# Operands of seven weight blocks made on GpSimd during attention, and the last rows' operands on GpSimd alone

## The chip, the cores and the metric

The kernel runs on one core of a Trainium2 chip. Times are device microseconds of a whole execution, "us" throughout. Engines are named as the profile names them: PE (TensorE matmul; PEld its weight loads), DVE (VectorE), ACT (ScalarE), POOL (GpSimd) and SP (SyncE, which here only issues transfers). "L970" is line 970 of the kernel before.

## The reference

One block of a transformer with 2048 rows of 576, modulated by a condition vector:

```python
mod = (silu(c) @ w_mod).reshape(1, 6, 1, -1)
sa, ca, ga, sb, cb, gb = (mod[:, 0], ..., mod[:, 5])
h = layernorm(x) * (1 + ca) + sa
x = x + ga * attention(h, wqkv, wo)      # 32 heads of 18, full softmax over 2048 keys
h = layernorm(x) * (1 + cb) + sb
g, u = h @ w_gate, h @ w_up              # 576 x 4608 each
return x + gb * ((sigmoid(g) * u) @ w_down)
```

Everything is float32.

## The kernel before, in words

**Precision by splitting.** Matrix products run on operands in the float32r type. An operand is split into a high part (a copy, rounded to float32r) and a low part (the operand less its high part), and a product is the sum of high x high, high x low and low x high. Much of ACT's, DVE's and POOL's work is such splitting.

**Stages.** First come layer norm and the projections to q, k and v. Then attention: 32 units, each a pair of heads for one half of the query rows (16 units a half), and 16 steps to a unit, so 512 steps. A step has matmuls for the row maxima of units to come, reduced on DVE (`maxima`, L415); score matmuls, whose exponentials ACT takes (L881); and value matmuls (`values`, L501). At a unit's end ACT copies the accumulated output to a buffer `oT` (`taken`, L515), PE transposes it, and POOL scales it into the row tile (`outputs`, L544).

The order in which a step's work is issued is written out by hand (`STEPS`), and during attention PE follows the program's order exactly (`manual_schedule`, L841). Other work is spread over the steps by generators, each advanced by one piece with `next`:

- `down_parts` (L775), steps 64 to 240: POOL multiplies each block of `w_down` by the gate vector, splits it and stores it in DRAM (`wds`).
- `first_rows`, steps 240 to 437: the output projection of the first 1024 rows, their second layer norm, and their operands for the gated unit, on POOL (`operand_parts`).
- `last_rows_project`, from step 437: most of the output projection of the last 1024 rows.

A load issued in these generators is tied with `paced` to the exponential of the step in which it stands, so that it doesn't start earlier.

**The gated unit.** Gate and up weights are taken in 18 blocks of 256 columns. A block's four quarters (A11, A12, A21, A22: two halves of the inner dimension by two halves of the columns) enter seven products instead of eight, in the order `ORDER = (1, 6, 2, 7, 5, 4, 3)`; products 5, 6, 7 and 3 need sums and differences of quarters. Each product is 14 matmuls of 512 columns (`product`, L979), seven for gate and seven for up. The loop runs twice over the 18 blocks: first for the first 1024 rows, then for the last 1024. At the first two products of a block the block before is multiplied with its down weights (`down`, L1015, 48 matmuls each), and DVE adds the results into the row tile (L1019), which frees PE's accumulator.

In the first half of the rows every block's operands are made as it goes (`weights_operand`, three products ahead, `LOOK = 3`): SP loads the raw weights (`load_block`), POOL makes the sums (L959), ACT copies the high part (L970), DVE subtracts the low part (L971, and L972 for the 64 partitions of the last, narrow slice of the inner dimension), and SP stores the finished operand in DRAM (`ws`, L973). In the second half the operands are only loaded from `ws` (L949).

While the first half runs, `last_rows` (L1059) brings the last 1024 rows up to the same point, one piece at every second product: the rest of the output projection (`od` loaded, transposed, L1098 on PE, `x1d` stored), the second layer norm (rows loaded into `z`, transposed by L663, spilled to `hs`), and the operands of the seven products (`operand_parts`: four blocks `B` loaded from `hs`; POOL subtracts, L690; ACT copies the high part, L679; DVE subtracts the low part, L681 and L686; SP stores to `xs`). At the first half's last block these operands replace the first half's in SBUF.

Up to product 56 (`ORDERED`) of the gated unit the framework's scheduler chooses PE's order, and after it the program's order holds. Each engine works through its queue in order, and so does each queue that issues transfers.

Of the kernel before, what the change touches and what calls it, by code (L numbers as in the profile page):

```python
# [23 lines left out]
P = 128  # L24
# [19 lines left out]
NB = F // 256  # L44
LAG = 2
# [6 lines left out]
def tile_block(ctx, tc, x_in, wqkv, wo, w_gate, w_up, w_down, c_in, w_mod, out):  # L52
# [33 lines left out]
    def load_mod(a, b, i):  # L86

        cols = slice(2 * D * i, 2 * D * (i + 1))
        for t in range(0, 4, 2):
            rows = slice(t * P, (t + 2) * P)  # L90
            nc.sync.dma_start(a[:, t : t + 2, :], w_mod[rows, cols].rearrange("(t p) c -> p t c", p=P))
        nc.sync.dma_start(b[0:64, :], w_mod[DM:D, cols])
        return [a[:, t, :] for t in range(4)] + [b]
# [218 lines left out]
    with tc.tile_pool(name="ln", bufs=2) as ln:  # L312
# [23 lines left out]
        with tc.tile_pool(name="wmp", bufs=1) as wmp:  # L336
            zs = normalized(0)
            wm = wmp.tile([P, 5, 2 * D], F32, name="wm")
            wm = load_mod(wm[:, 0:4, :], wm[:, 4, :], 0)
# [147 lines left out]
    bgp = bgs.enter_context(tc.tile_pool(name="bgp", bufs=1))  # L487
# [320 lines left out]
    def load_block(pool, b, k, tied=None):  # L808
# [4 lines left out]
        raw = pool.tile([P, 2, 3, 256], F32, name=f"raw{k}", bufs=1 + k)  # L813
        queue = nc.gpsimd if tied else nc.sync
# [10 lines left out]
        return raw  # L825
# [18 lines left out]
    downs = down_parts()  # L844
    for u in range(UNITS):
# [6 lines left out]
        for kt in range(NT):  # L852
# [31 lines left out]
            if u in (1, 3):  # L884
                if kt == 2:
                    a = big.tile([P, 8, 640], F32, name="big")
                    a = a.rearrange("p a b -> p (a b)")[:, 0 : 8 * D].rearrange("p (t c) -> p t c", t=4)
                    b = slots.tile([P, 2560], F32, name="w0")[:, 0 : 2 * D]
                    mods = load_mod(a, b, 1 + u // 2)
                    row = slots.tile([P, 2560], F32, name="w1")[:, 0:384]  # L890
# [4 lines left out]
            if 4 * NT <= step < FROM0 and step % 2 == 0:  # L895
                next(downs, None)
            if step == FROM0:
                for _ in downs:
                    pass
# [5 lines left out]
            if u == 30 and kt == 7:  # L905
                first = [load_block(raws, 0, k, paced) for k in range(2)]
# [4 lines left out]
            if u == UNITS - 1 and kt == 9:  # L911
# [5 lines left out]
                for i in range(2):  # L917
                    X[5 + i] = both[:, i]
                    load_x(5 + i)
    while pending:  # L920
        values()
# [20 lines left out]
    def weights_operand(st, k):  # L942
# [3 lines left out]
        kept = ws[st["b"], ORDER.index(k)]  # L946
        flat = w.rearrange("p v a c -> p (v a c)").bitcast(F32)
        if st["half"] == 1:
            nc.sync.dma_start(flat, kept.bitcast(F32))  # L949
            return  # L950
# [10 lines left out]
        if k == 6:  # L961
            put("S1", A21, A22, ALU.add)
            put("S2", st["S1"], A11, ALU.subtract)
# [267 lines left out]
```

## Time and profile before

| | us |
|---|---|
| median of three runs | 2938.05 |
| lowest, highest | 2929.16, 2941.33 |
| the profiled execution | 2936.12 |
| its span, first to last instruction | 2934.3 |
| PE busy | 2867.2 |
| DVE busy | 2305.1 |
| ACT busy | 1497.6 |
| POOL busy | 614.7 |

The profile is of one execution. Its page gives busy time by engine, the span in 40 slices, the queues of the transfers, the chain of work that ended last, and the costliest groups of instructions. The trace behind it answers for any stretch, line or tile. Busy time of PE is modelled, since matmuls overlap; a group's mean is the mean duration of one instruction, which may overlap the next one's, so that count by mean is more than the busy time. In a chain of waits each row is a start, a length and what the time went to.

### The profile page before, as it was taken

The numbers are of one execution on the slowest core, as the hardware profiler recorded it, in microseconds if no ns is written. First come the engines' busy times: TensorE is split into PE (matmuls) and PEld (weight loads), VectorE is DVE, ScalarE is ACT, GpSimd is POOL, SyncE is SP. The second block draws the span as 40 slices with busy tenths as digits, with TensorE's granted clock in tenths as the row PEclk, the third lists the DMA queues.
The fourth block names the chain that finished last, engine by engine and source line by source line (L and its number), as shares of the span: only waits on it lengthen the run. The fifth ranks groups of instructions, "written<-read, shape, count | busy, mean of one in ns | idle before, by whom it ended". The sixth has DMA issues, their size and how long they took to land.

```text
span 2934.3 us, 46129 instructions
## 1 busy us (share of the span) xinstructions
PE 2867.2 (98%) x17141; PEld 1884.6 (64%) x17141; DVE 2305.1 (79%) x4021; ACT 1497.6 (51%) x2779; POOL 614.7 (21%) x793
## 2 busy tenths in 40 slices
PE   7999999999999999999999999998999999999999
PEld 6974333333334443443443788887888888888888
DVE  7278999999999999999992778888777555555555
ACT  3217778888887678878778333333332111111111
POOL 2001024444213110661102222233221100000000
PEclk9999999999999999999999999999999999999999
DMA  5333113333212110221125866686556854444443
GB/s 170 119 138 115 63 58 134 126 116 112 83 50 70 31 50 19 95 92 60 48 78 185 280 217 231 232 278 242 204 201 225 303 177 168 166 168 169 158 158 137
DMA packets 136089, 420.25 MB, mean 143 GB/s; under 512 B 18805, under 2 KB 56441, under 8 KB 123577
## 3 DMA queue, kind: packets, MB, share of 16 engines
q1 hardware_dynamic: 120472, 338.35, 33.7%
q0 software_dynamic: 15392, 78.95, 7.6%
q8 instruction: 135, 2.21, 0.3%
q14 instruction: 90, 0.73, 0.1%
HBM read 261.13 MB, written 155.59 MB: 142 GB/s over the span
## 4 chain that ended last, share of the span: by engine, by line
PE 85%; DVE 5%; ACT 4%; issue 3%; DMA 2%; SPq 1%; POOL 0%; ACTq 0%; DVEq 0%; POOLq 0%
PE o L501 17%; PE d L1015 14%; PE s L877 13%; PE x L979 13%; PE s L411 9%; PE bg L979 4%; PE bu L979 4%; PE s L267 4%; ACT p L881 3%; PE s L301 2%; PE s L638 2%; DVE w L971 1%; PE s L525 1%; DMA B<-hs 1%; DVE u L1163 0%
## 5 line engine op out<-in xcount | busy, mean ns | idle before, releaser
L415 DVE TENSOR_REDUCE mx<-s 128x1 f32<-128x512 f32 x2048 | 1266.9, 681 | 43.9 <-PE s L411 35.3
L881 ACT ACTIVATE p<-s 128x512 f32<-128x512 f32 x2048 | 1066.9, 607 | 268.7 <-PE s L411 145.4
L411 PE MATMUL s<-k,q 54*128 54x512 f32 x1920 | 658.0, 441 | 2.6 <-ACT p L881 1.0
L877 PE MATMUL s<-q,k 56*128 56x512 f32 x1920 | 581.5, 433 | 6.3 <-ACT p L881 0.4
L877 PEld LDWEIGHTS s<-q,k 56*128 56x128 f32 x1920 | 277.6, 185 | 469.5 <-DVE mx L415 292.6
L501 PE MATMUL o<-p,vaug 128*32 128x512 f32 x4096 | 554.4, 606 | 0.0
L1015 PE MATMUL d<-wd,hh 128*128 128x288 f32 x2304 | 470.9, 298 | 20.9 <-DVE Oa L1019 20.3
L1015 PEld LDWEIGHTS d<-wd,hh 128*128 128x128 f32 x2304 | 375.7, 189 | 35.8 <-DVE Oa L1019 27.2
L411 PEld LDWEIGHTS s<-k,q 54*128 54x128 f32 x1920 | 312.1, 185 | 80.5 <-ACT p L881 37.4
L1019 DVE TENSOR_TENSOR Oa<-Oa,d 128x288 f32<-128x288 f32 x576 | 255.9, 452 | 128.2 <-PE d L1015 123.1
L1015 PE MATMUL d<-wd,hl 128*128 128x288 f32 x1152 | 342.0, 297 | 0.0
L979 PE MATMUL x<-k,w 128*128 128x512 f32 x1008 | 245.5, 394 | 4.7 <-ACT w L970 2.4
L1015 PEld LDWEIGHTS d<-wd,hl 128*128 128x128 f32 x1152 | 218.1, 189 | 0.0
L979 PEld LDWEIGHTS x<-k,w 128*128 128x128 f32 x1008 | 188.8, 190 | 43.2 <-DVE u L1190 3.5
L991 ACT ACTIVATE u<-u 128x512 f32<-128x512 f32 x72 | 45.5, 631 | 318.7 <-DVE u L1179 312.7
L501 PEld LDWEIGHTS o<-p,vaug 128*32 128x32 f32 x4096 | 83.6, 108 | 163.7 <-issue 147.7
L988 ACT ACTIVATE sg<-x 128x512 f32<-128x512 f32 x36 | 21.5, 598 | 309.4 <-PE x L979 309.4
L1021 POOL DMA_DIRECT2D out_dram<-Oa x16 | 8.7, 542 | 606.5 <-DVE Oa L1019 606.5
L979 PE MATMUL x<-big,w 128*128 128x512 f32 x504 | 120.6, 390 | 1.0 <-issue 1.0
L979 PE MATMUL x<-w,w 128*128 128x512 f32 x504 | 121.0, 390 | 0.0
L267 PE MATMUL s<-hT,wq_h 128*128 128x512 f32 x324 | 106.1, 399 | 1.9 <-DVE hT L204 1.2
L979 PEld LDWEIGHTS x<-big,w 128*128 128x128 f32 x504 | 94.3, 188 | 21.0 <-issue 1.4
(221 smaller groups left out, 3345.2 us busy)
## 6 DMA issues: line engine op xcount, KB each, us to landing
ws<-w SPq DMA_DIRECT2D x126, 640.0 KB
w<-ws SPq DMA_DIRECT2D x126, 640.0 KB
wd<-wds SPq DMA_DIRECT2D x36, 1152.0 KB
wds<-w POOLq DMA_DIRECT2D x18, 1152.0 KB, 4.5
k<-qk SPq DMA_DIRECT2D x60, 288.0 KB
qk<-pl SPq DMA_DIRECT2D x32, 512.0 KB
w<-in_B_w_down_dram POOLq DMA_DIRECT2D x18, 576.0 KB, 4.9
q<-qk SPq DMA_DIRECT2D x64, 144.0 KB
```

The source lines that it names most:

```text
L267: nc.tensor.matmul(acc, w, hT[:, t, cols], start=n == 0, stop=n == len(ts_) - 1)
L301: nc.tensor.matmul(acc[:, 0:HALF], hT[:, k, rows], w, start=n == 0, stop=n == len(ts_) - 1,)
L411: nc.tensor.matmul(sp, qs[rows, qt * P : (qt + 1) * P], ks[rows, kc * 512 : (kc + 1) * 512], start=True, stop=True,)
L415: nc.vector.tensor_reduce(mx[:, h * n + qt, kc : kc + 1], sp, axis=AX.X, op=ALU.max)
L501: nc.tensor.matmul(acc[32 * j : 32 * j + 32, :], vaug[:, kt, (2 * p + h) * VW : (2 * p + h) * VW + 32], probs[2 * c + h], start=kt == 0, s ...
L638: nc.tensor.matmul(acc[:, :HALF], a, w, start=i == 0, stop=i == len(ts_) - 1)
L877: nc.tensor.matmul(sT, ks[rows, kcols], qs[rows, c * 512 : (c + 1) * 512], start=True, stop=True)
L881: state["exp"] = nc.scalar.activation(pr, sT, AF.Exp, scale=SCALE)
L979: nc.tensor.matmul(acc[v], w[:, v, a, :], X[s][:, b, :], start=first and n == 0, stop=n == 6, skip_group_check=not first,)
L991: nc.scalar.activation(t[:, 0:512], t[:, 0:512], AF.Sigmoid)
L1015: nc.tensor.matmul(acc[:, :HALF], a[:, f, rows], w[:, f, cols], start=n == 0, stop=n == 5)
L1019: nc.vector.tensor_add(Oa[:, t, cols], Oa[:, t, cols], acc[:, :HALF])
```

## The change

1. **Seven blocks' operands during attention** (`AHEAD = 7`). A new generator `operands()` runs on POOL, one operand at a piece: at every third step up to step 64, then at every sixth step up to 240. It loads a block's two raw tiles through POOL's queue into the room that `big` has before the second half's outputs need it, makes the sums, the high copy and both low subtractions on POOL, in a tile `w` of which there are two in turn, and stores to `ws`. In the gated unit the blocks 0 to 6 then load their operands in the first half of the rows too; the first three are loaded at the end of attention, into the raw tiles' room.
2. **Room for it.** The modulation weights (`load_mod`), which used `big`, go to `w0`, `w1` and a temporary. The pool `bgp` is opened at step 240 only; before that its place holds `opp`, with the operand tiles and a second `oT` for every other unit of the first half up to unit 12.
3. **Blocks 7 to 17.** The sum for product 7 is made at product 7 and no longer at product 6; the 64-partition subtraction moves from DVE to POOL.
4. **Last rows.** `operand_parts` runs on POOL alone, and its loads and stores are on POOL's queue; the loads are issued two turns before their use. The rows `xt` are loaded one ahead, and the loads of `z` a turn before the statistics. The pieces come at every product from 5 to 32 and then at two of three, where they came at every second.

The core of the diff:

```diff
+AHEAD = 7
...
-        oT = epool.tile([P, 512], F32, name="oT")
+        pool = opp if half == 0 and p % 2 and p < FROM0 // NT - 2 else epool
+        oT = pool.tile([P, 512], F32, name="oT")
...
+    def operands():
+        room = big.tile([P, 8, 640], F32, name="big").rearrange("p a b -> p (a b)")
...
+        def load(b, k):
+            if b < AHEAD:
+                fill_block(raw[k], b, k, nc.gpsimd, paced)
+        load(0, 0)
+        load(0, 1)
+        yield
+        for b in range(AHEAD):
+            for k, src, op, a, c in (
+                (7, S3, ALU.subtract, A11, A21), (1, A11, None, None, None),
+                (5, S2, ALU.add, A21, A22), (6, S2, ALU.subtract, S2, A11),
+                (3, S2, ALU.subtract, A12, S2), (2, A12, None, None, None), (4, A22, None, None, None),
+            ):
+                if op is not None:
+                    for v in range(2):
+                        nc.gpsimd.tensor_tensor(src[:, v], a[:, v], c[:, v], op=op)
+                w = opp.tile([P, 2, 5, P], F32R, name="w", bufs=2)
+                for v in range(2):
+                    nc.gpsimd.tensor_copy(w[:, v, 0:3, :], src[:, v])
+                for rows, t, to in ((slice(0, P), slice(0, 2), slice(3, 5)), (slice(64, P), slice(2, 3), slice(2, 3))):
+                    nc.gpsimd.tensor_sub(w[rows, :, to, :], src[rows, :, t, :], w[rows, :, t, :].bitcast(F32))
+                nc.gpsimd.dma_start(
+                    ws[b, ORDER.index(k)].bitcast(F32), w.rearrange("p v a c -> p (v a c)").bitcast(F32)
+                )
+                if k in (6, 4):
+                    load(b + 1, k == 4)
+                yield
...
+            if step % 3 == 0 if step < 4 * NT else step < FROM0 and step % 6 == 1:
+                next(ops, None)
...
-            if u == 30 and kt == 7:
-                first = [load_block(raws, 0, k, paced) for k in range(2)]
...
+                for i, k in enumerate(ORDER[:LOOK]):
+                    w = raws.tile([P, 1536], F32R, name=f"raw{min(i, 1)}", bufs=1 + min(i, 1))[:, 0:1280]
+                    begun["w", k] = w.rearrange("p (v a c) -> p v a c", v=2, a=5)
+                    load_operand(begun["w", k], 0, k)
...
-        if st["half"] == 1:
-            nc.sync.dma_start(flat, kept.bitcast(F32))
+        if st["half"] == 1 or st["b"] < AHEAD:
+            load_operand(w, st["b"], k)
             return
...
+        elif k == 7:
             put("S3", A11, A21, ALU.subtract)
...
-        nc.vector.tensor_sub(w[64:P, :, 2, :], src[64:P, :, 2, :], w[64:P, :, 2, :].bitcast(F32))
+        nc.gpsimd.tensor_sub(w[64:P, :, 2, :], src[64:P, :, 2, :], w[64:P, :, 2, :].bitcast(F32))
...
-                    xt = pool.tile([P, D], F32, name="xt", bufs=2)
-                    nc.sync.dma_start(xt, x1p[:, t0 + j, :])
+                    xt = xs_[j]
+                    if j < 3:
+                        xs_.append(load_x1(pool, t0 + j + 1))
...
-                    ln_stats(zp, x1, mv2[:, t, :])
                     zs.append(z)
+                yield
+                for j, z in enumerate(zs):
+                    ln_stats(zp, z[:, :, 0:HALF], mv2[:, 4 * ch + j, :])
...
-                    nc.sync.dma_start(t, hs[g, i, :, cols])
-                yield from operand_parts(1, i, blocks, parts, nc.scalar.copy, nc.vector, nc.sync)
+                    nc.gpsimd.dma_start(t, hs[g, i, :, cols])
+                yield
+                yield
+                yield from operand_parts(
+                    1, i, blocks, parts, nc.gpsimd.tensor_copy, nc.gpsimd, nc.gpsimd
+                )
...
-        if n >= 5 and n % 2:
+        if 5 <= n < 33 or n >= 33 and n % 3:
             next(rows2, None)
```

More of the change, by code (lines that the diff above doesn't have):

```diff
@@ L1025, in tile_block @@
     seq = [(half, b, k) for half in range(2) for b in range(NB) for k in ORDER]
-    blocks = {}
+    blocks = {(0, 0): begun}
     def load(i, k):
-        if i < NB and (i, k) not in loaded:
-            loaded[i, k] = load_block(raws, i, k)
-    loaded = {(0, k): first[k] for k in range(2)}
+        if AHEAD <= i < NB and (i, k) not in loaded:
+            loaded[i, k] = raws.tile([P, 2, 3, 256], F32, name=f"raw{k}", bufs=1 + k)
+            fill_block(loaded[i, k], i, k, nc.sync)
+    loaded = {}
     def block(n):
```

70 lines of the change are left out of this document (44 added, 26 removed).

## The prediction

> **What bounds the kernel now.** I read the page's head first, then busy time by stretches, then the chain of waits inside the blocks of the gated unit.
>
> ```profile
> span 2934.3 us, 46129 instructions
> PE 2867.2 (98%) x17141; PEld 1884.6 (64%) x17141; DVE 2305.1 (79%) x4021; ACT 1497.6 (51%) x2779; POOL 614.7 (21%) x793
> ```
>
> PE is nearly never idle and POOL mostly is. The profiled execution took 2936.12 us, span 2934.3 and 1.8 around it; the median of the three runs is 2938.05, so 1.9 more. A share over the whole span hides stages, so next come the gated unit's stretches, cut where a block of seven products (98 product matmuls each) begins: blocks 0-6, 7-11 and 12-17 of the first half of the rows, then the second half. First the product matmuls alone (stretch, length, PE busy, PE weight loads, granted clock, DMA share, GB/s), then all engines (PE, weight loads, DVE, ACT, POOL).
>
> ```profile
> 1602.80:1868.20 265.40, 166.31 (x686) 128.85 (x687) 0.99 0.71 246
> 1868.20:2067.40 199.20, 114.42 (x492) 91.12 (x491) 0.97 0.72 252
> 2067.40:2284.80 217.40, 135.29 (x589) 109.63 (x589) 1.00 0.60 217
> 2284.80:2914.10 629.30, 406.06 (x1765) 328.95 (x1764) 1.00 0.50 176
> ```
>
> ```profile
> 1602.80:1868.20 265.40, 256.85 (x1390) 222.52 (x1391) 210.29 (x390) 90.77 (x132) 68.11 (x67) 0.99 0.71 246
> 1868.20:2067.40 199.20, 185.05 (x988) 161.82 (x987) 165.15 (x268) 71.14 (x110) 65.53 (x52) 0.97 0.72 252
> 2284.80:2914.10 629.30, 629.30 (x3493) 559.93 (x3492) 350.64 (x613) 108.79 (x181) 9.15 (x17) 1.00 0.50 176
> ```
>
> The second half runs 18 blocks in 629.30 us, 34.96 each, with PE idle for nothing and DVE busy 56%: that is PE's own pace, with operands that only have to be loaded. Blocks 0-6 take 265.40, blocks 7-11 39.8 each, and DVE is busy about 80% there. The chain of waits shows what PE's pace is made of, and how a block of the first half that makes operands but carries no work for the last rows loses against it:
>
> ```profile
> 2111.67 1.29 DVE u L1163 x2
> 2112.96 0.36 DVE Oa L1019
> 2113.32 0.98 DVE w L971
> 2114.30 0.38 DVE Oa L1019
> ...
> 2114.72 3.60 PE d L1015 x24
> 2118.32 3.18 PE x L979 x14
> ...
> 2124.68 6.36 PE d L1015 x48
> ...
> 2161.14 6.36 PE d L1015 x48
> ```
>
> Fourteen product matmuls take 3.18 us and 48 down matmuls 6.36. A block is 7 x 3.18 + 2 x 6.36 = 34.98. From 2124.68 to 2161.14 is 36.46: 1.5 us lost, where DVE makes operands (L971) in front of the additions (L1019) that give PE its banks back. So the first half is bound by PE plus a DVE queue that runs late in each block. Blocks 0-6 and 7-11 also carry the last rows' projection, normalisation and operands.
>
> **The change part by part.**
>
> *Seven blocks' operands on GpSimd in attention.* This removes 49 of 126 ACT copies (L970) and DVE subtractions (L971, L972), and 56 of the sums (L959), from blocks 0-6, and adds the same work to POOL under attention. Rows for POOL's price:
>
> ```profile
> L959 POOL TENSOR_TENSOR S<-raw,raw 128x384 f32<-128x384 f32 x36 | 37.1, 1048 | 49.0 <-PE s L877 16.7 <-DVE w L972 10.7 <-issue 7.1
> L795 POOL CAST w<-w 128x288 fp32r<-128x288 f32 x72 | 28.4, 422 | 0.0
> L679 POOL CAST t<-t 128x512 fp32r<-128x512 f32 x14 | 8.5, 608 | 0.3 <-DMA xs<-t 0.2
> L681 POOL TENSOR_TENSOR t<-t,t 128x512 fp32r<-128x512 f32 x9 | 11.6, 1284 | 0.4
> L626 POOL TENSOR_TENSOR t<-t,t 64x128 fp32r<-64x128 f32 x8 | 3.6, 456 | 0.6
> L816 POOL DMA_DIRECT2D raw<-in_B_w_up_dram x2 | 1.5, 736 | 0.0
> ```
>
> An operand needs two casts of 384 columns (between 0.42 and 0.61, say 0.50 each), a subtraction of 512 columns (1.28), one of 256 on 64 partitions (between 0.46 and 0.64, half of 1.28; with a start cost in it I take 0.7) and a store's issue (taken as a load's, 0.74): 3.7 us. Four of seven have two sums of 1.05 as well: 5.8. A block is 3 x 3.7 + 4 x 5.8 = 34.3, plus eight load issues of 0.74, so 40.2; seven blocks 281 us. What hides it is POOL's idleness from the first step to the first rows' work:
>
> ```profile
> 237.00:400.00 163.00, 15.81 (x12) 0.99 0.21 69
> 400.00:842.00 442.00, 169.94 (x274) 1.00 0.31 107
> POOL w L794 <- DMA w<-in_B_w_down_dram: 79.2, 18, 7.4
> L566 POOL DMA_DIRECT2D t<-in_A_wo_dram x4: 577/578/600, 860.7 to 884.2; - x4
> L605 PE MATMUL s<-ident,Oa x32: 272/273/330, 914.8 to 1085.3; 128*128 128x128 f32 x32
> ```
>
> POOL is busy 186 of these 605 us and waits 79 for down weights; with 281 more that is 546, and the first work that PE waits for starts at 860.7. The waits that come with it (each load paced by an exponential, each second operand buffer waiting for its store) hold only POOL's queue; behind them stand the down weights, which nobody reads before the gated unit, and the attention outputs (L544), whose buffer now alternates between two in the first half. Do the other engines feel it? In attention DVE's main work is the maximum (L415):
>
> ```profile
> L415 DVE TENSOR_REDUCE mx<-s x2048: 639/681/694, 139.8 to 1550.1; 128x1 f32<-128x512 f32 x187
> ```
>
> Its longest of 2048 is 694 ns though POOL worked beside many of them, so I put attention at 0. If that cover were gone, up to 281 us would be at stake. The change of load_mod's buffers, the temporaries' turn and the three loads that replace the raw loads at the end of attention go at 0 too: these three start six steps before attention's end, some 16 us at (1602.8 - 237) / 512 = 2.7 a step, before their reader.
>
> *Start of the gated unit.*
>
> ```profile
> 1602.88 5.04 PE L979 MATMUL x<-k,w 128*128 128x512 f32 x14 [2.38 <-ACT w L970]
> ```
>
> The first product waits 2.38 us for an operand that the change has in SBUF already. Bounds 0 and -2.4; the last outputs still free their bank on DVE, so I take -1.5.
>
> *Blocks 0-6.* Floor: products and downs 22.26 + 6 x 34.98 = 232.1 (block 0 has no downs). The last rows' PE work now all falls into blocks 0-4, since its steps come at each product up to the 33rd:
>
> ```profile
> 1652.70 1.32 PE d L1098 x10
> 1885.59 0.44 PE d L663 x4
> 1632.59 7.11 DMA od<-oend
> 1759.36 4.87 DMA z<-x1d
> ```
>
> Eight rows at 1.32 and 64 transposes (48 of L663, 16 of L1075 and L1082) at 0.11 are 17.6. The floor is 249.7, now 265.4. What stays above it: these steps wait for loads (od was 7.1 us on the chain, z 4.9), and a step now comes one product after the load where it came two after. The two prefetches (xt, and z a turn ahead) help against that. Bounds 0 and 24 (both od and both z in full, 2 x 7.1 + 2 x 4.9); I take 9, nearer the low end, because DVE and ACT are as free there as in the second half, and the DMA queues, which now move 246 GB/s, get the second half's operand loads (176 in all) instead of weights in and operands out: 258.7, so -6.7 (bounds -15.7 and +8).
>
> *Blocks 7-11.* The last rows' operands leave ACT, DVE and SP (L679, L681, L686) for POOL, their loads two turns ahead on POOL's queue.
>
> ```profile
> 1960.51 6.60 DMA B<-hs
> ...
> 2016.40 9.23 DMA xs<-ho
> ```
>
> These waits on the chain stood in ACT's and DVE's queues ahead of PE's operands; now at worst POOL waits. What is late next is the 36.46 of a block that makes operands. POOL pays per put 0.61 + 1.28 + 0.75, about 3.4 with its share of the sums, on two of three products: beside the block's eight sums and seven small subtractions some 30 of 36 us, so I add 0.3: 5 x 36.8 = 184 against 199.2: -15 (bounds -24, at 34.96, and 0).
>
> *Blocks 12-17, and 7-11 again: the small subtraction moved from DVE to POOL.*
>
> ```profile
> L972 DVE TENSOR_TENSOR w<-S,w 64x256 fp32r<-64x256 f32 x72 | 31.2, 433 | 1.3
> 2144.68 2.44 POOL L959 TENSOR_TENSOR S<-raw 128x384 f32<-128x384 f32 x2 [5.32 <-issue]
> 2144.78 1.47 DVE L995 TENSOR_TENSOR hl<-u,hh 128x512 fp32r<-128x512 f32 x1 [0.23 <-ACT hh L994]
> 2146.18 1.49 DVE L971 TENSOR_TENSOR w<-S,w 128x512 fp32r<-128x512 f32 x1
> ```
>
> Five of them, 2.1 us, stand in DVE's queue before the late additions, more than the 1.5 lost. But two DVE subtractions beside POOL's sums took 1.47 and 1.49, where they take 0.69 elsewhere: some 0.8 each is lost to POOL. On POOL the small one costs about 0.7, and it starts with L971, both behind the same ACT copy. So between -1.5 and +1.45 a block (5 x (0.72 - 0.43)); I take -0.4, six times: -2.4 (bounds -9 and +9).
>
> The Trainium skill's page "SBUF — State Buffer" (Who interferes with whom) says that a VectorE instruction with two SBUF inputs and a GpSimd one that reads SBUF exclude each other, the second waiting for the whole of the first. By that rule these two rows are the rule and not a mishap, each moved subtraction can cost DVE more than it spares, and the sum is the first rival's.
>
> Sum: -1.5 - 6.7 - 15 - 2.4 = -25.6; 2936.12 - 25.6 = 2910.5, so 2911.
>
> **The rivals.** *POOL takes back what it relieves.* If each small subtraction delays L971 by its whole 0.72, blocks 7-17 lose 1.5 + 1.45 and run at 37.9: 11 x 37.9 = 417, against 199.2 + 217.4 = 416.6 now. Only start and blocks 0-6 gain: 2936.1 - 8.2 = 2928. For it speak 1.47 and 1.49; against it that much of what DVE does there reads a bank of PSUM, like L415, which POOL doesn't touch.
>
> *The last rows' steps come too close.* The seven blocks lose nothing worth having to operands, and the denser steps pay all of the 24 us above the floor: 15 more than I took, 2926. Against it: the steps' order on PE is left to the scheduler before the 56th product, so they can move behind their loads.
>
> *POOL is late out of attention (the slower side).* The place is step 240, where the first rows' work begins. The weights' preparation there, five tiles with two two-input instructions and a cast of 576 columns (by the rows above 1.6, 1.6 and 0.8), takes POOL 20 us of the 54 between 860.7 and 914.8, so 34 are spare. From 237 to 860.7 are 624 us; POOL has 624 + 34 - 186 - 79 = 393 for the new work. It decides if that takes over 1.4 times my 281; at 1.6 times (450) PE stands for 57 us: 2968. For it: a sum cost 1.05 by the row that I used, but 1.22 (half of 2.44) beside DVE. Against it: 1.22 for 1.05 is far from 1.4 on everything.
>
> *It does all that it says.* Every block at PE's pace: -2.4 - 15.7 - 24.4 - 7.6 = -50, 2886.
>
> **How the numbers follow.** The forecast, between 2893 and 2923, has 0.65; POOL taking back 0.11; steps too close 0.14; POOL late 0.06; everything at PE's pace 0.04. A measurement of this kernel can tell 0.5%, 15 us, from no change. Below 2923 lie forecast, full gain and a little of the two middle rivals: faster 0.71; within, the rest of these two: 0.22; slower: POOL late and a rest, 0.07. The range leaves out the full gain's lower part and POOL late, and takes in both middle rivals with some scatter: 2889 to 2935.
>
> **What would show it.** Right: the first product starts between 1599 and 1604; POOL's busy time from 237 to 842 rises from 186 by some 230 (issues are not all counted); L415 stays at 681; no L970 in blocks 0-6, which take about 259; blocks 7-11 under 37.5 each with no wait of ACT or DVE for B or xs; blocks 12-16 at or under 36.4; the second half still 629. Wrong: a wait of PE for POOL after step 240; L971 at 1.2 us and more on the mean; blocks 0-6 over 266 with od or z on the chain; POOL as the last releaser of operands in blocks 7-11.

## The result, and the profile after

The changed kernel is slower: 2983.0 us in the median of its runs (2973.74 to 2990.2), against 2934.61 for the kernel before (2929.16 to 2941.33). The ratio is 1.0162, with a 95% interval of 1.0125 to 1.0199. The forecast of 2911 us, faster, was wrong by 2.5%.

The profiled execution is the fastest of those runs, 2973.74 us, 37.6 above the profiled one of before; the other three took 8.2 to 16.5 us more, with mean granted clocks of 0.979 to 0.983 against its 0.984. Its page begins:

```profile
span 2972.0 us, 46195 instructions
PE 2865.6 (96%) x17141; PEld 1884.8 (63%) x17141; DVE 2198.8 (74%) x3818; ACT 1448.8 (49%) x2709; POOL 966.3 (33%) x1245
```

The work did move: POOL is busy 352 us more, DVE 106 less, ACT 49 less, and PE as long as before. (Line numbers are now those of the changed kernel: the maximum is L416, the copies of the outputs L517 and L542, their scaling on POOL L546, the sums L1010, the product L1033 and the small subtraction L1024.) The same stretches of the gated unit, all engines (length; PE, weight loads, DVE, ACT, POOL; granted clock, DMA share, GB/s):

```profile
1641.00:1894.00 253.00, 252.01 (x1406) 221.60 (x1407) 154.91 (x289) 58.05 (x89) 65.89 (x77) 1.00 0.73 244
1894.00:2107.60 213.60, 179.47 (x972) 158.32 (x971) 130.26 (x207) 57.45 (x86) 120.18 (x113) 0.91 0.58 199
2107.60:2317.60 210.00, 210.00 (x1166) 186.58 (x1165) 153.25 (x246) 67.01 (x101) 92.44 (x86) 1.00 0.64 225
2317.60:2949.00 631.40, 629.59 (x3494) 560.21 (x3493) 350.85 (x613) 108.99 (x181) 9.16 (x17) 1.00 0.50 176
```

Against before: the gated unit starts at 1641.0 instead of 1602.8, 38 us late. Blocks 0-6 take 253.0 instead of 265.4, with PE idle for 1 us. Blocks 7-11 take 213.6 instead of 199.2, with PE idle for 34 and a mean clock of 0.91. Blocks 12-17 take 210.0 instead of 217.4: six blocks at exactly PE's pace of 35.0. So the relief of the blocks came as meant; two losses outweigh it.

**The first loss: POOL's lateness in attention.** Up to about 570 us every unit starts within 0.5 us of its time before; then the delay grows at single units, to 38 at the end. The waits of the changed kernel from 238 to 860 us (engine and line, what it waited for, total us, times, longest):

```profile
POOL w L796 <- DMA w<-in_B_w_down_dram: 65.1, 15, 7.7
POOL big L849 <- DMA big<-in_B_w_gate_dram: 51.6, 9, 8.9
...
DVE rec L531 <- POOL Oa L546: 28.2, 3, 12.6
ACT oT L542 <- DVE rec L531: 26.9, 3, 12.2
...
PE s L412 <- ACT oT L542: 25.3, 3, 11.6
```

The last three lines are one chain, three times. One link of it in the timeline, from 576 to 592 us, with ACT's copy (L542) of the unit before ahead of it (start, length, engine, line, in square brackets what it waited):

```profile
537.67 0.62 ACT L542 COPY oT<-s 128x512 f32<-128x512 f32 x1
...
576.91 0.66 PE L527 MATMUL s<-ident,oT 128*128 128x128 f32 x4
...
589.65 0.81 POOL L546 TENSOR_TENSOR Oa<-oT,rec 128x144 f32<-128x144 f32 x2
590.50 0.26 DVE L531 RECIPROCAL rec<-s 128x16 f32<-128x16 f32 x1 [12.63 <-POOL Oa L546]
590.85 0.59 ACT L542 COPY oT<-s 128x512 f32<-128x512 f32 x1 [12.18 <-DVE rec L531]
...
591.49 0.79 PE L412 MATMUL s<-k,q 54*128 54x512 f32 x1 [11.64 <-ACT oT L542]
```

PE has transposed a unit's output at 577.6. DVE now wants to write its reciprocals into `rec`, which has one buffer, and POOL has not yet scaled the output of the unit before with the old ones: it does so at 589.65, some 51 us after that copy, where a unit lasts 41. Everything behind the reciprocal, the next maxima included, waits. Until POOL is more than a unit late, nothing of this costs anything; from then on each further us costs PE about one. And a stall is followed by a second loss (stretch, length, PE busy, granted clock, DMA share, GB/s):

```profile
575.00:584.00 9.00, 4.85 (x34) 1.00 0.50 171
584.00:601.00 17.00, 9.51 (x40) 0.50 0.40 143
601.00:615.00 14.00, 13.85 (x90) 0.99 0.57 184
```

The clock is granted at half for 17 us, more than nine of them after work has begun again. Three stalls of 25.3 us in all and a wait of 2.3 for a transfer (`q<-mrows`) make 27.6 of the 38. The rest is put down to the slower clock behind these four: PE worked 28 us at half clock there, where eight matmuls of L502 took 1.93 us and otherwise 1.06, so by estimate up to some 13 us.

Why POOL is late, in three stretches of attention (POOL busy, with its issues):

```profile
237.00:400.00 163.00, 126.04 (x158) 1.00 0.57 180
400.00:600.00 200.00, 149.35 (x221) 0.96 0.48 165
600.00:842.00 242.00, 174.10 (x261) 0.94 0.45 153
```

449.5 us of work in 605, and 130 of waits for transfers (65.1, 51.6, and 12.9 for the operand buffer's store): some 25 us are left, so POOL catches up only slowly once it is late.

**The second loss: block 7.** It takes 73.6 us where 8 to 17 take 35.0. POOL's timeline there:

```profile
1909.40 2.57 POOL L688 TENSOR_TENSOR ho<-B,ho 32x512 fp32r<-32x512 f32 x2
1912.04 0.61 POOL L681 CAST ho<-B 128x512 fp32r<-128x512 f32 x1
1912.59 0.56 POOL L689 DMA_DIRECT2D xs<-ho  x1
1913.21 0.72 POOL L1024 TENSOR_TENSOR w<-raw,w 64x256 fp32r<-64x256 f32 x1
...
1934.05 0.56 POOL L689 DMA_DIRECT2D xs<-ho  x1 [0.30 <-POOL ho L688]
1934.68 0.72 POOL L1024 TENSOR_TENSOR w<-S,w 64x256 fp32r<-64x256 f32 x1
1935.47 1.97 POOL L1010 TENSOR_TENSOR S<-raw,S 128x384 f32<-128x384 f32 x2
```

L681 to L692 are the last rows' operands, which nobody needs before the first half's last block. POOL works through all of them from 1823 to 1934 us. The first of block 7's small subtractions (L1024) stands among the last of them, at 1913.21; the next ones and the block's next sum (L1010) stand behind them all. PE feels it twice (waits from 1890 to 1970):

```profile
PE x L1033 <- POOL w L1024: 18.3, 1, 18.3
...
PE bg L1033 <- POOL w L1024: 15.8, 1, 15.8
```

### The profile page after: what moved, and what is told of

Read it like the earlier page. It is cut to its first block, busy times and chain, and to the rows that moved or that the text cites. A ratio compares the mean times of both kernels' runs of the same rounds, so it can differ in the third digit from the quotient of the medians.

```text
span 2972.0 us, 46195 instructions
## 1 busy us (share of the span) xinstructions
PE 2865.6 (96%) x17141; PEld 1884.8 (63%) x17141; DVE 2198.8 (74%) x3818; ACT 1448.8 (49%) x2709; POOL 966.3 (33%) x1245
## 3 DMA queue, kind: packets, MB, share of 16 engines
q0 software_dynamic: 31360, 132.87, 12.8%
## 4 chain that ended last, share of the span: by engine, by line
PE 77%; POOL 10%; DMA 6%; ACT 3%; issue 2%; DVE 1%; SPq 0%; POOLq 0%; ACTq 0%; DVEq 0%
PE d L1069 14%; PE x L1033 14%; PE o L502 12%; PE s L918 10%; PE s L412 7%; PE bu L1033 5%; PE bg L1033 5%; PE s L268 4%; DMA w<-in_B_w_down_dram 3%; PE s L302 2%; ACT p L922 2%; PE s L640 2%; POOL w L796 2%; POOL w L798 2%; POOL w L854 1%
## 5 line engine op out<-in xcount | busy, mean ns | idle before, releaser
L416 DVE TENSOR_REDUCE mx<-s 128x1 f32<-128x512 f32 x2048 | 1266.6, 681 | 54.2 <-PE s L412 45.7
L412 PE MATMUL s<-k,q 54*128 54x512 f32 x1920 | 664.4, 445 | 28.1 <-ACT oT L542 25.3
L918 PE MATMUL s<-q,k 56*128 56x512 f32 x1920 | 588.2, 437 | 8.8 <-DMA q<-mrows 2.3
L502 PE MATMUL o<-p,vaug 128*32 128x512 f32 x4096 | 559.2, 611 | 0.0
L1069 PE MATMUL d<-wd,hh 128*128 128x288 f32 x2304 | 460.8, 295 | 0.3 <-DVE Oa L1073 0.3
L1033 PE MATMUL x<-k,w 128*128 128x512 f32 x994 | 240.8, 393 | 18.3 <-POOL w L1024 18.3
L1033 PEld LDWEIGHTS x<-k,w 128*128 128x128 f32 x994 | 185.1, 189 | 55.6 <-POOL w L1024 18.7
L502 PEld LDWEIGHTS o<-p,vaug 128*32 128x32 f32 x4096 | 83.9, 108 | 164.8 <-issue 148.9
L1033 PE MATMUL x<-big,w 128*128 128x512 f32 x504 | 120.8, 390 | 0.0
L1033 PE MATMUL x<-w,w 128*128 128x512 f32 x490 | 117.1, 390 | 0.0
L1033 PEld LDWEIGHTS x<-big,w 128*128 128x128 f32 x504 | 94.6, 188 | 19.4
```

The costliest lines, as they stand in the source:

```text
L412: nc.tensor.matmul(sp, qs[rows, qt * P : (qt + 1) * P], ks[rows, kc * 512 : (kc + 1) * 512], start=True, stop=True,)
L416: nc.vector.tensor_reduce(mx[:, h * n + qt, kc : kc + 1], sp, axis=AX.X, op=ALU.max)
L502: nc.tensor.matmul(acc[32 * j : 32 * j + 32, :], vaug[:, kt, (2 * p + h) * VW : (2 * p + h) * VW + 32], probs[2 * c + h], start=kt == 0, s ...
L918: nc.tensor.matmul(sT, ks[rows, kcols], qs[rows, c * 512 : (c + 1) * 512], start=True, stop=True)
L1033: nc.tensor.matmul(acc[v], w[:, v, a, :], X[s][:, b, :], start=first and n == 0, stop=n == 6, skip_group_check=not first,)
L1069: nc.tensor.matmul(acc[:, :HALF], a[:, f, rows], w[:, f, cols], start=n == 0, stop=n == 5)
```

## The experiments

The times behind each are medians, the ratio stands against the kernel before, run on the same chip; terms by stretch come from the profiled execution of each. Edits are to the changed kernel unless said otherwise.

**1. The small subtraction back on DVE.**

```diff
-        nc.gpsimd.tensor_sub(w[64:P, :, 2, :], src[64:P, :, 2, :], w[64:P, :, 2, :].bitcast(F32))
+        nc.vector.tensor_sub(w[64:P, :, 2, :], src[64:P, :, 2, :], w[64:P, :, 2, :].bitcast(F32))
```

> The changed kernel with one line undone: the 64-partition subtraction of blocks 7 to 17 is on DVE again. In the changed kernel PE stood 18.3 and 15.8 us in block 7 (73.6 us long) for that instruction, 0.72 us of work behind the last rows' operands in POOL's queue. Theory: that alone is the wait; block 7 falls to 36-40 us and the kernel gains about 35 us on the changed one, near 2948, still slower than before because attention still ends 39 us late. Rival: POOL as a whole is late there, and the sums for the block's last products come late in its place; block 7 stays over 50 us and the gain is under 25. Second question, the 35.0 us of blocks 8 to 17 (36.5 before): if the moved subtraction bought them, they go back to 36.3-36.6; if not, they stay at 35.0.

Measured: 2993.41 us, 1.0205 (1.019 to 1.0221). Block 7 still takes 67.3 us, and blocks 8 to 16 take 36.5 instead of 35.0. Waits from 1905 to 1980 us:

```profile
PE d L1069 <- DVE Oa L1073: 29.0, 4, 27.1
ACT w L1022 <- POOL S L1010: 26.9, 1, 26.9
```

So it is not this subtraction that was put badly: the sums, which POOL made before too, wait in the same queue. And in the blocks where POOL has time, the moved subtraction is worth 1.5 us a block. This run's first product started at 1656.5, later than the 1641.1 of the same attention code above: when the lateness passes a unit differs between executions.

**2. More buffers for POOL's late scaling.** The reciprocals in three buffers, the outputs in three in turn.

```diff
-            pool = opp if half == 0 and p % 2 and p < FROM0 // NT - 2 else epool
-            oT = pool.tile([P, 512], F32, name="oT")
+            if half == 0 and p % 3 and p < FROM0 // NT - 2:
+                oT = opp.tile([P, 512], F32, name="oT", bufs=2)
+            else:
+                oT = epool.tile([P, 512], F32, name="oT")
...
-        rec = epool.tile([P, 4, 4], F32, name="rec")
+        rec = epool.tile([P, 4, 4], F32, name="rec", bufs=3)
```

> The changed kernel with room for POOL to be late in attention: three buffers for rec, where there is one, and three for oT in the first half, where there are two. Theory: what stopped PE was DVE's reciprocal (12.9, 5.9 and 10.3 us at three unit ends) waiting for the one rec buffer that POOL still had to read; with three the waits go, and the first product of the gated unit starts at 1602-1610 where it started at 1641, the kernel gains 30 to 39 us, near 2948. Rival: POOL has more work up to step 240 than time, so the wait only moves, to oT or to the first rows' projection after step 240, and the first product still starts after 1630, no gain over 10. Block 7 stays at 73 us by both.

Measured: 2969.97 us, 1.0131 (1.0116 to 1.0146); between the medians that is 13 us less than the changed kernel, and under 5 between the profiled executions. The three stalls are gone, and the lateness now grows unhindered, from 23 us at the first unit to 81 at the twelfth. Then the outputs' own buffer is the one not free; one wait takes the place of three (238 to 860 us):

```profile
ACT oT L519 <- POOL Oa L548: 29.8, 1, 29.8
```

The first product starts at 1636.7. The loss moved, as the rival had it; that POOL lacks the time, its reason, experiment 10 refutes.

**3. Both of these edits.**

> Both edits in one kernel. Theory: the two waits are independent and the gains add: 2983 - 35 - 35 = 2913, or 2927 if blocks 8 to 17 go back to 36.4 us. Rivals: as in the two runs alone; if POOL's whole queue is the trouble in both places, the sum stays over 2950.

Measured: 2976.92 us, 1.0154 (1.0132 to 1.0175); start 1639.9, block 7 67.8, blocks 8 to 16 at 36.5. The start is about that of experiment 2 and the blocks are those of experiment 1; the expected sum of two gains did not come.

**4. Five blocks ahead instead of seven**, the later parts at every eighth step instead of every sixth.

```diff
-AHEAD = 7
+AHEAD = 5
...
-            if step % 3 == 0 if step < 4 * NT else step < FROM0 and step % 6 == 1:
+            if step % 3 == 0 if step < 4 * NT else step < FROM0 and step % 8 == 1:
```

> The changed kernel with less work on POOL in attention: five blocks instead of seven, and after step 64 one operand at every eighth step instead of every sixth, so 80 us less before step 240, with the same single rec buffer. Theory (POOL's lateness): the waits at unit ends go, the first product starts at 1602-1606, although the DMA traffic and everything else of the change stay. Rival (the added DMA traffic, or the DVE and POOL port, and not POOL's queue): over half of the 39 us stays. In the gated unit the first block that makes its own operands is now block 5, so the wait for the small subtraction moves there: by the theory one of the blocks 5 to 7 is over 60 us long.

Measured: 2963.91 us, 1.011 (1.0092 to 1.0128). POOL is busy 375.5 us instead of 449.5 in the same 605, its lateness peaks at 45.2 us, just over a unit, and the start is 1621.0: half of the loss is gone. But now blocks 5 and 6 make their own operands beside the last rows, and blocks 6 and 7 take 61.8 and 62.8 us. With the first parts spread as well (every fourth step):

```diff
-            if step % 3 == 0 if step < 4 * NT else step < FROM0 and step % 6 == 1:
+            if step % 4 == 0 if step < 4 * NT else step < FROM0 and step % 8 == 1:
```

> Five blocks in attention, and the operands spread more evenly: one at every fourth step up to step 64 (every third in the change), then one at every eighth. The run with five blocks at the old pace to step 64 still lost 18 us, at the two unit ends where POOL's scaling of the outputs came over 40 us after the copy that it waits for. Theory: POOL stops the others only when it is more than a unit (41 us) late; with the even pace its lateness stays under 30 us, and the first product starts at 1602-1608. Rival: what costs is each burst of raw loads beside the small transfers of the maxima, whatever POOL's lateness; then at least 10 us stay. In the gated unit as with five blocks before: blocks 6 and 7 over 55 us each.

Measured: 2962.31 us, 1.0104 (1.0083 to 1.0125). The early lateness falls (12.8 and 0.1 us at the second and third unit, from 27.4 and 33.7 with seven blocks), its peak later does not (45.8), and the start is 1620.0. Spreading the early parts alone bought nothing that counts.

**5. POOL in the order of the program from product 33 on.** The framework's scheduler chooses the order on every engine whose order is not fixed; this fixes POOL's as PE's is.

```diff
+        if n == 33:
+            manual.enter_context(tc.manual_schedule(engines={mybir.EngineType.Pool}))
...
-            manual.enter_context(tc.manual_schedule(engines={mybir.EngineType.PE}))
+            manual.enter_context(
+                tc.manual_schedule(engines={mybir.EngineType.PE, mybir.EngineType.Pool})
+            )
```

> The changed kernel with POOL's queue held to the program's order from the 33rd product on, as PE's is from the 56th; nothing else. In the changed kernel the scheduler put all three rounds of the last rows' operands ahead of the first small subtraction of block 7, in the program only the first round stands before it. Theory (order): block 7 falls from 73.6 to 36-40 us, the blocks after it stay at or under 37, and the kernel gains 30 to 38 us on the changed one. Rival (amount): POOL hasn't the time for the last rows and the blocks together, so the loss is spread over blocks 7 to 10, and their sum stays over 165 us (178.6 in the changed kernel).

Measured: 2968.36 us, 1.0124 (1.0109 to 1.0139). Block 7 falls to 35.0, and blocks 8 to 10 rise to 43.0, 41.8 and 40.5. From the start of block 7 to the end of block 10 (all engines):

```profile
1901.80:2062.10 160.30, 147.94 (x778) 130.85 (x777) 109.62 (x165) 45.30 (x68) 125.16 (x122) 0.95 0.63 229
```

160.3 us, where the changed kernel takes 178.6 and PE's pace would be 140. So about half of block 7's loss was the order, and both expectations missed: it is neither the order alone nor the amount alone. The other half is the amount, since POOL is busy 125 of 160 us there, and ACT and POOL wait for each other in turn (waits from 1900 to 2065 us):

```profile
POOL w L1024 <- ACT w L1022: 27.5, 18, 3.7
...
ACT w L1022 <- POOL S L1010: 17.8, 7, 6.2
```

**6. The last rows' operands on ACT, DVE and SP again**, the rest of the change kept.

```diff
-                    nc.gpsimd.dma_start(t, hs[g, i, :, cols])
+                    nc.sync.dma_start(t, hs[g, i, :, cols])
...
-                yield from operand_parts(
-                    1, i, blocks, parts, nc.gpsimd.tensor_copy, nc.gpsimd, nc.gpsimd
-                )
+                yield from operand_parts(1, i, blocks, parts, nc.scalar.copy, nc.vector, nc.sync)
```

> The changed kernel with the last rows' operands back on ACT (high parts), DVE (low parts) and SP (transfers), their loads still two turns ahead; POOL keeps its subtractions between blocks. Theory: POOL's queue is then short and block 7 takes 36-38 us; blocks 5 to 9 may pay some us each for ACT's and DVE's added work; net gain on the changed kernel 25 to 38. Rival (the small subtraction on POOL is late by itself, whatever else POOL does): block 7 stays over 60.

Measured: 2960.04 us, 1.0098 (1.0083 to 1.0113). Blocks 5, 6 and 7 take 38.6, 37.4 and 44.8 and all others from 8 on 35.0; the first half comes to 653.1 us, from 676.7. Moving the last rows' operands to POOL was a loss by itself, and most of it came from the order: with POOL in the program's order (experiment 5) the first half takes 657.5. The start, 1655.1, is as late as ever.

**7. The kernel before, with nothing but part 3** (the sum for product 7 made at product 7, the small subtraction on POOL).

```diff
+        elif k == 7:
             put("S3", A11, A21, ALU.subtract)
...
-        nc.vector.tensor_sub(w[64:P, :, 2, :], src[64:P, :, 2, :], w[64:P, :, 2, :].bitcast(F32))
+        nc.gpsimd.tensor_sub(w[64:P, :, 2, :], src[64:P, :, 2, :], w[64:P, :, 2, :].bitcast(F32))
```

> The kernel before with the smallest part of the change alone: the 64-partition subtraction on POOL, the sum for product 7 made at product 7. Undoing that line in the changed kernel took blocks 8 to 16 from 35.0 back to 36.5 us. Theory: here too blocks 12 to 16 go from 36.5 to 35.0, the blocks with last rows' work gain about as much, and the kernel is 8 to 25 us faster than before: 2907 to 2924. Rival (POOL and DVE exclude each other, so it helps only where POOL has nothing else to do): blocks 0 to 11 stay as they are or get longer, and the whole is within 8 us of before.

Measured: 2926.66 us, 0.9981 (0.9972 to 0.9991). Blocks 12 to 17 take 210.0, at PE's pace, without any other part of the change. The gain in the median is small beside the 0.5%; in the profile's blocks it is the whole 7.6 us that these blocks had to give. The expected 8 to 25 us did not come: the medians are 4.5 apart.

**8. Three blocks ahead, the last rows on the other engines, `rec` in two buffers.** The parts of an operand come at every fourth step and then at every sixteenth; the last rows' edit is that of experiment 6.

```diff
-AHEAD = 7
+AHEAD = 3
...
-        rec = epool.tile([P, 4, 4], F32, name="rec")
+        rec = epool.tile([P, 4, 4], F32, name="rec", bufs=2)
...
-            if step % 3 == 0 if step < 4 * NT else step < FROM0 and step % 6 == 1:
+            if step % 4 == 0 if step < 4 * NT else step < FROM0 and step % 16 == 1:
```

> What it is: the changed kernel with three blocks made ahead in attention instead of seven (the parts of an operand every fourth step in the first head pair and every sixteenth after it), the small tile of reciprocals in two buffers, and the last rows' operands made by ScalarE, VectorE and SyncE again. Theory (the loss is GpSimd's work in attention, and its last rows' work in blocks 7 to 9): GpSimd's added work in attention falls from 264 us to about 113 (3 of 7), so no exponential comes later than in the kernel before by more than 2 us and the first product starts at 1601 to 1606 us; the first-half blocks, with the small subtraction on GpSimd, come to 650 to 662 us in all against 682.3 before; the whole takes 2900 to 2915 us, less than both kernels. Rival (blocks 3 to 8, which now make their own gate and up operands beside the last rows, lose again what the spreading gains): start as above, but the first-half blocks at 675 to 685 us and the whole at 2925 to 2937. Second rival (the burst of raw loads, not GpSimd's amount, delays attention): start at 1612 us or later.

> What it is: the three-block kernel of the run before, with GpSimd's instructions from product 33 on in the order of the program. Theory (with the last rows off GpSimd there is nothing left that comes ahead of a block's small subtraction out of turn): start and blocks as in the run before within 3 us, the time within 0.3% of it. Rival (the order of GpSimd's own sums, sums of the down product and subtractions still costs in the blocks that make their operands): the first-half blocks 5 to 15 us shorter than in the run before.

Measured: 2921.84 us, 0.996 (0.9948 to 0.9972), and with POOL in the program's order 2922.71 us, 0.9966 (0.9954 to 0.9979). POOL is busy 300.0 us in attention (114 more than in the kernel before), its lateness is 25.5 us at most and under 6 from the sixth unit on, and the first product starts at 1604.4: attention loses nothing. The first half takes 668.9 and 669.8 us, between the two expectations: blocks 3 to 8 take 41.0 each on the mean, since these now carry their own operands and the last rows'. Four things differ here at once, so this pair shows what they do together and not what each is worth. Fixing POOL's order neither helps nor harms once the last rows are off it.

**9. Less POOL arithmetic with the same transfers.** The low parts are subtracted for the first two operands alone, into two fixed tiles; so the low parts of the operands of blocks 0 to 6 are left out, while every cast, load and store stays.

```diff
-                w = opp.tile([P, 2, 5, P], F32R, name="w", bufs=2)
+                w = both[made % 2]
+                made += 1
...
-                    nc.gpsimd.tensor_sub(w[rows, :, to, :], src[rows, :, t, :], w[rows, :, t, :].bitcast(F32))
+                    if made <= 2:
+                        nc.gpsimd.tensor_sub(w[rows, :, to, :], src[rows, :, t, :], w[rows, :, t, :].bitcast(F32))
```

> What it is: the changed kernel with the two subtractions that make the low parts of an operand done for the first two operands alone (two fixed tiles in turn), so the low parts of blocks 0 to 6 are left out; all casts, loads and stores stay. GpSimd does about 95 us less arithmetic in attention, and moves the same bytes with as many DMAs. Theory (the amount of GpSimd's work makes its output scaling late): the lateness stays under a unit of 41 us, no exponential is held by more than 3 us, and the first product starts at 1602 to 1610 us; block 7 still takes 70 to 76 us, since the order of GpSimd's work there is unchanged; the whole at 2940 to 2955 us. Rival (the loads and stores, in bursts, hold attention): the start stays at 1620 us or later.

Measured: 2940.57 us, 1.0028 (1.0018 to 1.0038). POOL is busy 356.0 us; the lateness stays under a unit but for one, 44.8 us, and PE waits once instead of three times (238 to 860 us):

```profile
DVE rec L531 <- POOL Oa L546: 6.1, 1, 6.1
ACT oT L542 <- DVE rec L531: 5.7, 1, 5.7
...
PE s L412 <- ACT oT L542: 5.1, 1, 5.1
```

The start is 1606.8 and block 7 takes 73.8. The bytes moved are the same, so it is the amount of POOL's work, by way of its lateness, that delays attention and not the bursts of transfers.

**10. The whole change, with room for the lateness.** Seven blocks ahead, four buffers each for the outputs and the reciprocals, the last rows as in experiment 6, from which it differs in these buffers alone.

```diff
-            pool = opp if half == 0 and p % 2 and p < FROM0 // NT - 2 else epool
-            oT = pool.tile([P, 512], F32, name="oT")
+            if half == 0 and p % 4 and p < FROM0 // NT - 1:
+                oT = opp.tile([P, 512], F32, name="oT", bufs=3)
+            else:
+                oT = epool.tile([P, 512], F32, name="oT")
...
-        rec = epool.tile([P, 4, 4], F32, name="rec")
+        rec = epool.tile([P, 4, 4], F32, name="rec", bufs=4)
```

> What it is: the changed kernel with all seven blocks made in attention, the head outputs in four buffers (three of them in the attention pool) and the reciprocals in four, and the last rows' operands made by ScalarE, VectorE and SyncE again. Theory (GpSimd's work does fit into the time between 237 and 860 us, and it is the lateness beyond the buffers' reach, with the last rows on GpSimd, that turns it into a loss): the output scaling runs up to 80 us late, four units of 41 us cover that, no unit is held by more than 5 us, and the first product starts at 1602 to 1612 us; the first-half blocks come to 650 to 656 us, as with the last rows on the other engines alone; the whole at 2902 to 2918 us, below both kernels. Rival (the wait moves once more, to the step where GpSimd's work for the first rows begins at 860 us): start at 1620 us or later, with a wait of TensorE on GpSimd's first-rows operands, and the whole at 2920 or more.

Measured: 2910.18 us (2909.39 to 2913.78), 0.9929 (0.9915 to 0.9942): faster than both kernels and than every other version here, and some 50 us less than experiment 6. Its gated unit starts at 1608.9; the stretches:

```profile
1608.90:1866.80 257.90, 252.96 (x1406) 221.78 (x1407) 165.94 (x309) 67.27 (x105) 32.64 (x31) 1.00 0.77 256
1866.80:2051.70 184.90, 178.70 (x972) 158.47 (x972) 137.87 (x216) 59.93 (x91) 86.76 (x77) 0.98 0.60 208
2051.70:2261.90 210.20, 210.20 (x1166) 186.58 (x1165) 153.07 (x246) 66.96 (x101) 91.92 (x86) 1.00 0.64 224
```

POOL is busy 442.7 us in attention, nearly as long as in the changed kernel (449.5), and up to 81.0 us late with its scaling; no wait for that is left there, because four buffers reach over three units. It is on time again for the first rows: no wait of PE for POOL shows between 860 and 1000 us. Of the 6 us at the start that remain, most lie around 620, where a matmul waits 3.1 us for the small transfer `q<-mrows` and the clock drops once more:

```profile
613.00:625.00 12.00, 9.14 (x49) 0.72 0.67 216
```

## Why the prediction was wrong

By its own terms, for the profiled execution: the start was to gain 1.5 us and lost 38; blocks 0-6 were to gain 6.7 and gained 12.4; blocks 7-11 were to gain 15 and lost 14.4; blocks 12-17 were to gain 2.4 and gained 7.4. What follows block 17 came out 5 us longer: 2 in the first block of the second half, 3 at the end.

**Attention at 0: the failed step.** The price was right. Here are its groups in the changed kernel (237 to 860 us; count, busy, mean ns, idle before it):

```profile
L854 POOL TENSOR_TENSOR w<-big,w 128x512 fp32r<-128x512 f32 x49 | 62.6, 1279 | 2.3
...
L849 POOL TENSOR_TENSOR big<-big 128x384 f32<-128x384 f32 x56 | 55.7, 1002 | 54.6 <-DMA big<-in_B_w_gate_dram 51.6 <-DMA big<-in_B_w_up_dram 1.9
L852 POOL CAST w<-big 128x384 fp32r<-128x384 f32 x98 | 47.3, 503 | 14.6 <-DMA ws<-w 12.9
L854 POOL TENSOR_TENSOR w<-big,w 64x256 fp32r<-64x256 f32 x49 | 35.6, 729 | 3.7
...
L855 POOL DMA_DIRECT2D ws<-w x49 | 27.8, 567 | 9.0 <-POOL w L854 8.3 <-issue 0.6
```

With 41.6 us for 56 load issues these make 271, against the 281 forecast. L416 stayed at 681 ns in its median and 694 at most, with POOL at work for three quarters of the time from 237 to 842 us, so DVE did not pay, as argued:

```profile
L416 DVE TENSOR_REDUCE mx<-s x2048: 627/681/694, 140.8 to 1589.7; 128x1 f32<-128x512 f32 x187
```

(The Trainium skill's page "SBUF — State Buffer", Who interferes with whom, says that this kind of instruction never contends with GpSimd on this chip; the row agrees.) What failed is the test that turned 281 into nothing. It pooled the spare time, 393 us up to 860.7, and asked whether the sum would fit. The sum fits: experiment 10 ends on time with the same work. But the outputs have to be scaled once a unit, and the queue runs in order, so what counts at each unit is how far POOL is behind at that unit against what the buffers bear. The prediction came close to it: "the attention outputs (L544), whose buffer now alternates between two in the first half" stand behind these waits. It counted `oT`, with two buffers, and not `rec`, which L544 reads beside it and which has one. In the kernel before POOL scaled most units' outputs within 3 us of ACT's copy and none later than 10.1, so its trace did not show the limit; only the program did. The waits were undercounted as well: "hold only POOL's queue" left them out of the sum, and 64.5 us for raw loads and stores stand there (51.6 and 12.9), beside the 65.1 for down weights that it had at 79.

**Blocks 7-11: the second failed step.** "Beside the block's eight sums and seven small subtractions some 30 of 36 us" took POOL's work as spread over the blocks in the program's order. The scheduler laid nearly all of it ahead of block 7's. Experiment 5 puts the order right and gets 18 of the us back; the other 20 over PE's pace remain. POOL is busy 31 us a block there (125.16 in four), so the 30 was right in size, and the "0.3" that was added for it was not: these four blocks take 40.1 each, against 36.8 forecast. On an engine with so little left, PE's operands wait for whatever is in front of them. Experiment 6 takes the last rows off POOL and gives 184.7 us for blocks 7-11, against the 184 forecast, though by the other way: ACT, DVE and SP carry the last rows, mostly beside blocks that have no operands to make. "POOL as the last releaser of operands in blocks 7-11" was among the prediction's signs of being wrong, and it came.

**What held.** Blocks 0-6 came to 253.0 against a floor worked out at 249.7; the 9 us taken for denser steps were 3. Blocks 12-17 of the changed kernel and of experiment 7 answer the first rival: the small subtraction takes longer beside DVE than in attention (means of 0.95 and 1.06 us in blocks 12-17, 0.73 for the same shape in L854 above), but POOL has this time, and DVE's large one does not pay for it (L1023 takes 0.97 us on the mean there, L971 took 0.96). Experiment 1 prices the move at 1.5 us a block in its favour, where the forecast had 0.4. (The Trainium skill's page "SBUF — State Buffer", Who interferes with whom, says that a VectorE instruction with two SBUF inputs contends with a GpSimd one that reads SBUF; the longer small subtraction agrees.) The rival on the slower side named the right engine, late in attention, with the wrong place: PE waits for POOL nowhere between step 240, where it was put, and the gated unit. It also had the wrong deciding point: 1.4 times 281 us were not needed.

With room for the lateness and the last rows off POOL, experiment 10 comes near the forecast's terms: start 1608.9 (1601.4 forecast), blocks 0-6 257.9 (258.7), 7-11 184.9 (184), 12-17 210.2 (215), and 2910 us for the whole (2911). That the whole fits to 1 us is in part luck: a start 7.5 us late is partly made up by blocks 12-17, 4.8 better; the 184.9 is not reached by the forecast's way; and the profiled execution, from which these terms come, took 2913.78. So the forecast described what the idea can bring, and not this version of it.

## What to carry to other kernels

Work put on an idle engine is hidden only as long as the engine's regular duty is never later than the buffers between it and its neighbours reach; ask for every tile that duty reads how many buffers it has, and compare the lateness at each turn with them, not the sum of the work with the sum of the idle time. Work that is not urgent must not share an in-order queue with work that is, unless its order there is fixed, and even then the time must suffice where it falls due (experiment 5). Where the amount fits and only the moments do not, more buffers can turn the loss into a gain: here two more of the outputs, 2 KB a partition each, and three more of the small reciprocals took 46 us off the start of the gated unit (experiments 6 and 10).

## What the runs showed of the hardware

The cost of a stall of PE is longer than the stall. During and after each of the three in attention, and the two in block 7, the granted clock stood at 0.50 for 6.8 to 20.5 us, of which 3.8 to 9.6 us came after PE had begun again. It fell to 0.50 at a gap of 2.3 us as well (the wait for `q<-mrows`, 667.6 to 669.9) and stayed there until 679.7. The Trainium skill's page "TensorE: Matmul & The Clock Gate" (What's actually happening) gives the half clock after about 3.4 us of idleness and its end after about 3.4 us of sustained work. The five stalls, of 4.7 to 18.3 us, agree with the first figure and the gap of 2.3 does not; the second does not fit, since PE began again at 591.5 and was busy for all of the 9.5 us up to 601 at half clock.

A load that POOL issues for its own use stands on its path when it runs late: in attention it waited 24 times for down weights and raw gate weights, 4.9 us on the mean (116.7 / 24) and up to 8.9.
